# First heads' scores over 66 rows, the first scan and its rows issued ahead of other fills, a table load and the first weights' load

## The chip, the cores and the metric

One Trainium2 chip, one core of it. The time is device microseconds of one execution of the program; before and after are compared by the median of their runs. The profile is of one further execution. Engines: PE (TensorE: MATMUL, and PEld for its weight loads), DVE (VectorE), ACT (ScalarE), POOL (GpSimd), SP (SyncE, which issues most DMAs; rows with SPq or ACTq are DMA issues).

## What is computed

Causal attention with a forget gate (4 batches, 8 heads, 576 positions, 64 wide), then two feed-forward layers on its 2304 rows of 512, each of 2048 hidden columns. Cut to what matters:

```python
scores = matmul(q, k.T) / sqrt(D)
cum    = cumsum(log(clip(f, 1e-4, 1.0)), axis=-1)
scores = where(causal, -1e9, scores + cum[:, None] - cum[None, :])
x      = softmax(scores) @ v          # heads side by side: [2304, 512]
x      = square(relu(x @ w_in)) @ w_out
h      = x @ w_in2
x      = where(h >= 1, h, where(h <= -1, 0, (h + 1)**2 / 4)) @ w_out2
```

## The kernel before

The 2304 columns are worked off in four blocks of 512 to 640. Block 0 holds the first 256 positions of batches 0 and 1. Its heads are taken four at a time: a *group* (`attention32`; groups 0 to 3 make block 0, 4 to 7 block 1). For a group, K and Q of four heads lie transposed in a tile `QK` (two buffers, used in turn): partitions 0 to 63 hold the 64 dimensions, row D = 64 holds cum on the K side and -8 on the Q side, row D + 1 holds 8 on the K side and cum on the Q side, so the score matmul (L819, `s0q` for group 0) adds the decay by itself. All 128 partitions are contracted; the rows beyond are 8 on the K side and 0 on the Q side. These constants are written by `clear` (L726): by DVE for the first buffer, by POOL for the second, in two halves each.

The cum rows come from `setup`: load f (L599), clamp (L603, DVE), Ln (L605, ACT), scan (L607, DVE), each in two pieces, columns 0 to 255 and 256 to 575. Then `first_rows` (L647) copies the first scan's result to rows D and D + 1 of group 0's tile, one DMA on SP's queue and one on ACT's; other groups read it back from DRAM (`cumd`, L642 and L793). ACT loads the table of Exp (L611) after the Ln. A run of matmuls on the identity (L713, `warm`), whose result nobody reads, stands on PE before the scores.

After the scores: masked maximum on DVE (L764, `E0q`), Exp on ACT (L830), scaling by the sum (L853 ACT, L854 DVE), transposes (`tr0q`, L862), products with V (`av0q`, L876), and x written in two float16 pieces (L741, L744, L758).

The feed-forward weights come as 64-bit floats. Each piece of weights (`raw`, L1302; the first two, `raw-2` and `raw-1`, are half pieces) is decoded to float32 by ACT and DVE (L1332, L1336, L1341, L1343), split into two float16 parts (L1398 on ACT or L1399 on DVE, then L758; tile `whl`), and stored for later (`scr`, L1405). The first layer's matmuls are L1423 (`h`), the second's L1587 to L1589 (`acc`).

No order is written out by hand. Every operation is given to a planner with a due time, a guessed cost per engine and, for loads, an earliest time; `Schedule.run` plays the operations through with these costs and picks for each engine the one that is due first, and some operations may go to either of two engines. `improve` repeats this for several weights of the engines' costs and keeps the order with the smallest guessed end; that order is emitted. So a change of one due time can move instructions anywhere. The numbers in two lists are earliest times: `QE` for the groups' QK loads, `RE` for the first raw loads, and `WARM` is the number of warm matmuls.

Of the kernel before, what the change touches and what calls it, by code (L numbers as in the profile page):

```python
# [16 lines left out]
AF = mybir.ActivationFunctionType  # L17
ALU = mybir.AluOpType

B, H, S, D = 4, 8, 576, 64  # L20
DM, DFF = 512, 2048
NT = B * S
P = 128
# [12 lines left out]
HEAD = 256  # L36
# [18 lines left out]
QUAD = 4  # L55
# [1 line left out]

SLAV = [0.0, 0.51, 1.3, 1.3]
SLQK = [0.0, 0.271, 0.412, 0.414]
QE = [0.0, 5.4, 8.66, 11.6]  # L60
VE = [5.5, 6.1]
RE = [1.36, 7.73, 16.0]
LW = 29.1
WARM = 17


def pattern(bits):
# [63 lines left out]
TURN = 0.05  # L131
LEAD = 15.4

WEIGHTS = [{"DVE": x, "POOL": x / 2} for x in (0.4, 0.5, 0.6, 0.8, 1.0)]

class Buf:
    def __init__(self, pool, make, kind=None):
# [25 lines left out]
class Schedule:  # L163
# [175 lines left out]
    def improve(self, pools, rounds):  # L339
        first = [o.due for o in self.ops]  # L340
        best = None
        for weight in WEIGHTS:
            for o, f in zip(self.ops, first):
# [48 lines left out]
def dma_t(nbytes, dram=True, late=0.0):  # L392
    issue = 0.45 if dram else 0.625
    size = nbytes / 380e3
    return issue, size, issue + 0.03, late + 0.1 + 0.35 * size
# [19 lines left out]
def tile_attention_moe_moe(ctx: ExitStack, tc: tile.TileContext, qkv, f, w2, outT, halves, seen=None, bad=None):  # L415
# [19 lines left out]
    sch = Schedule()  # L435
# [35 lines left out]
    def new(tag, name, shape=None, dt=None, kind=None):  # L471
        p, _, sh, d, _ = pools[tag]
        shape = sh if shape is None else shape
        kw = {"padded_shape": sh} if list(shape) != list(sh) and len(shape) == len(sh) and dt is None else {}

        def make():
            if pools[tag][1] is None:
                late_pools()
            return pools[tag][1].tile(shape, dt or d, tag=tag, name=name, **kw)

        return Buf(p, make, kind)
# [8 lines left out]
    else:  # L490
# [13 lines left out]
         early=True)  # L504
# [81 lines left out]
    QK = [new("PT", f"QK{i}", [P, QUAD * 2 * HEAD], F32) for i in range(2)]  # L586
# [3 lines left out]
    def setup():  # L590
        sb = new("xb", "setup", [P, 4 * S], F32)
        fr, lf, cum = (lambda i=i: sb.tile[:H * B, S * i:S * i + S] for i in range(3))
        onesf = lambda: sb.tile[:H * B, 3 * S:4 * S]
        due = -100.0
        G, V_, A = nc.gpsimd, nc.vector, nc.scalar
        tiny_op.append(sch.op(due - 9, {"POOL": (0.05, lambda: G.memset(tiny, 2.0 ** -30))}))
        oh = sch.op(due - 200, {"POOL": (0.05, lambda: G.memset(warm, 0.5))})
        oh = sch.op(due - 200, {"ACT": (1.5, lambda: A.activation(warm, warm, AF.Ln))}, [oh])
        o1 = sch.op(due, {"SP": (dma_t(73728), lambda: nc.sync.dma_start(out=fr(), in_=f))}, bufs=[sb], early=0.0)  # L599
        o2 = sch.op(due - 5, {"POOL": (0.55, lambda: G.memset(onesf(), 1.0))}, bufs=[sb])  # L600
        sch.op(due + 90, {"POOL": (0.05, lambda: G.memset(half, 0.5 * sh[1] ** 0.5))})
        cut = [slice(0, HEAD), slice(HEAD, S)]
        o3 = [sch.op(due, {"DVE": (0.15 + 0.1 * i, lambda c=c: V_.tensor_scalar(  # L603
            fr()[:, c], fr()[:, c], 1e-4, 1.0, op0=ALU.max, op1=ALU.min))}, [o1], [sb]) for i, c in enumerate(cut)]
        o4 = [sch.op(due, {"ACT": (0.32 + 0.05 * i, lambda c=c: A.activation(lf()[:, c], fr()[:, c], AF.Ln))}, [o3[i], oh], [sb])  # L605
              for i, c in enumerate(cut)]
        scan = lambda c, x: V_.tensor_tensor_scan(  # L607
            cum()[:, c], onesf()[:, c], lf()[:, c], x(), op0=ALU.mult, op1=ALU.add)
# [73 lines left out]
        if not halves:  # L682
            due = -30.0
# [7 lines left out]
        if halves:  # L691
# [5 lines left out]
            fill=1.0, base=0, channel_multiplier=1))}, [i1])  # L697
        return o7, zs, ms, i2, o8, first_rows, rows_of_pairs

    cum_op, zs, mask_op, id_op, cumd_op, first_rows, rows_of_pairs = setup()  # L700
    def new_x(name, blk):
        sh = [P, NKC, 2, WIDTH[blk]]
# [4 lines left out]
    def warm_up():  # L707
# [3 lines left out]
        def mms(n):  # L711
            for _ in range(n):
                nc.tensor.matmul(ps.tile[:, :P], ident, ident, start=True, stop=True)  # L713

        sch.op(-90, {"PE": (0.36 * WARM, lambda: mms(WARM))}, [id_op], [ps])

    warm_up()

    def clear(i, half):

        n = QUAD * HEAD
        rows = lambda a, z: QK[i].tile[a:z, n * half:n * half + n]
        kq = lambda a, z, t: rows(a, z).rearrange("p (c t n) -> p c t n", t=2, n=HEAD)[:, :, t, :]
        due = -98 + 2 * i + half
        eng, m = ("POOL", nc.gpsimd) if i else ("DVE", nc.vector)
        fill = lambda out, x: {eng: (n / 1920 + 0.03, lambda: m.memset(out(), x))}  # L726
        kr = sch.op(due, fill(lambda: kq(D, P, 0), 8.0), [], [QK[i]])
        qr = sch.op(due, fill(lambda: kq(D, P, 1), 0.0), [], [QK[i]])
        return [kr, sch.op(due, fill(lambda: kq(D, D + 1, 1), -8.0), [qr], [QK[i]])]

    cleared = {(i, half): clear(i, half) for i in range(2) for half in range(2)}


# [34 lines left out]
    def attention32(g):  # L768
# [1 line left out]
        first = g.blk == 0  # L770
        qk, n = QK[g.i % 2], QUAD * 2 * HEAD
        reg = lambda: qk.tile
        kr = lambda c: reg()[:, 2 * c * HEAD:2 * c * HEAD + HEAD]
        qr = lambda c: reg()[:, 2 * c * HEAD + HEAD:2 * c * HEAD + 2 * HEAD]
        wait = groups[g.i - 2].qk if g.i >= 2 else ()
        src = qkv[g.at:g.at + D * n].rearrange("(p n) -> p n", p=D)
        loads, parts = [], 2 if g.i == 0 else 1
        for i in range(parts):
            c = slice(n // parts * i, n // parts * (i + 1))
            loads.append(sch.op(g.due - 6, {"SP": (dma_t(P * n * 4 // parts), lambda c=c: nc.sync.dma_start(  # L780
                out=reg()[:D, c], in_=src[:, c]))}, wait, [qk], early=QE[g.i] if g.i < len(QE) else None))
        row = g.b * H + g.h
        place = lambda t, c0, c1: reg()[D + t:D + t + 1].rearrange("p (c t n) -> p c t n", t=2, n=HEAD)[:, c0:c1, t, :]
        ready = []
        for i in range(parts):
            c0, c1 = QUAD * i // parts, QUAD * (i + 1) // parts
            if parts == 2:
                if i == 0:
                    rows = [first_rows(row, lambda t=t: place(t, 0, QUAD), -90, [*cleared[0, 0], *cleared[0, 1]], ("SP", "ACT")[t])
                            for t in range(2)]  # L790
                ready += [[loads[i], *rows]] * (c1 - c0)
            else:
                rows = [sch.op(g.due - 4, {"SP": (dma_t(4096), lambda t=t, c0=c0, c1=c1: nc.sync.dma_start(  # L793
                    out=place(t, c0, c1), in_=cumd[row + c0:row + c1, :].rearrange("(o c) n -> o c n", o=1)))},
                    [cumd_op, *wait, *cleared[g.i % 2, 0], *cleared[g.i % 2, 1]], [qk]) for t in range(2)]
                ready += [[loads[i], *rows]] * (c1 - c0)
# [487 lines left out]
    def w_load(s):  # L1284
# [10 lines left out]
        if first:  # L1295
            b = new("raw" if halves else "big", f"raw{s}", [P, 2, 512], U64) if W64 else new("wf", f"wf{s}")
            loads = []
            for pair, layers in first.items():
# [4 lines left out]
                        out=b.tile[:, c], in_=w2[pair].rearrange("p (l n) -> p l n", l=2)[:, c]))},  # L1303
                    [], [b], early=RE[s + LAG] if s <= 0 else V0(s + 2) - 17 - LW))
                for layer in layers:
# [316 lines left out]
    def attend(blk):  # L1622
        if blk:
            xb[blk] = new_x(f"x{blk}", blk)
        for g in groups:
            if g.blk == blk:
                attention32(g)
        if blk in carry:
            buf, (_, off, c0, c1), deps = carry[blk]
            n = c1 - c0  # L1630
            split_x(blk, range(NKC), off, lambda: buf.tile[:, :, :n], n, deps, buf, V[NFC * ATTENTION[blk][0]] + 2)
        for t in tasks:
            if t.blk == blk:
                (attention_pair if halves else attention)(t)
# [600 lines left out]
```

## Time and profile before

| | us |
|---|---|
| median of 3 runs (lowest, highest) | 863.54 (862.9, 866.13) |
| the profiled execution, its own time | 864.67 |
| its span, first to last instruction | 862.8 |
| PE busy in the span | 845.9 (98%) |
| DVE busy | 763.6 (89%) |
| ACT busy | 605.3 (70%) |

A busy time counts the time in which at least one instruction of the engine is under way. Matmuls overlap, so the start of one to the start of the next is the price of one in a row of them, and the duration shown for one is longer than that.

### The profile page before, as it was taken

What the parts mean: (1) busy time and instruction counts of PE and PEld (TensorE: products, weight loads), DVE (VectorE), ACT (ScalarE), POOL (GpSimd) and SP (SyncE); (2) the same over time, 40 slices, a digit from 0 to 9 for tenths busy, and PEclk for the clock granted to TensorE, in tenths of its full rate; (3) what the DMA queues carried; (4) which work ended last, traced back from release to release, by engine and by line L of the source; (5) the groups of instructions that cost most, each with busy time, mean ns of one, the idle gap of its engine ahead of it and who ended that gap; (6) DMA issues with size and microseconds to landing.
All of it is one profiled execution on the core that took longest, in us unless ns stands there. A gap on an engine that the chain in (4) does not pass through costs nothing.

```text
span 862.8 us, 14696 instructions
## 1 busy us (share of the span) xinstructions
PE 845.9 (98%) x4930; PEld 462.7 (54%) x4930; DVE 763.6 (89%) x1882; ACT 605.3 (70%) x1232; POOL 23.8 (3%) x120
## 2 busy tenths in 40 slices
PE   8999999999999999999999999999999999999996
PEld 7644444454444444444446654466556556665553
DVE  8999999999789878989888789986899998999993
ACT  7999988996677667767577577756564566756652
POOL 3000004000000000000000000000000000000000
PEclk9999999999999999999999999999999999999999
DMA  8799997886599998699489988677464454335432
GB/s 258 210 319 323 353 346 230 275 279 222 164 270 226 255 218 241 150 229 257 164 227 264 256 237 208 158 191 161 129 198 156 159 171 159 109 112 168 139 112 76
DMA packets 144841, 180.68 MB, mean 209 GB/s; under 512 B 91670, under 2 KB 96918, under 8 KB 140726
## 3 DMA queue, kind: packets, MB, share of 16 engines
q1 hardware_dynamic: 144750, 179.67, 71.2%
q8 instruction: 40, 0.66, 0.3%
q14 instruction: 43, 0.35, 0.1%
q10 hardware_dynamic: 8, 0.00, 0.0%
HBM read 127.84 MB, written 30.81 MB: 184 GB/s over the span
## 4 chain that ended last, share of the span: by engine, by line
PE 76%; DVE 12%; ACT 6%; DMA 3%; issue 2%; SPq 0%; POOL 0%; DVEq 0%; POOLq 0%; ACTq 0%
PE h L1423 17%; PE acc L1587 8%; PE acc L1589 8%; PE acc L1588 8%; PE h L1972 6%; PE av L1246 3%; PE X L1837 3%; PE Y L1837 2%; PE b L1924 2%; PE b L1926 2%; PE b L1925 2%; DVE wf L1343 2%; PE s L1147 1%; PE s L1146 1%; DMA PT<-PP 1%
## 5 line engine op out<-in xcount | busy, mean ns | idle before, releaser
L1423 PE MATMUL h<-x,whl 128*128 128x512 f16 x912 | 214.3, 379 | 1.0 <-DVE g L1455 1.0
L1423 PEld LDWEIGHTS <-whl 128*128 128x128 f16 x912 | 88.0, 98 | 103.5 <-issue 3.9
L1587 PE MATMUL acc<-gh,whl 128*128 128x512 f16 x312 | 118.3, 379 | 0.0
L1589 PE MATMUL acc<-gl,whl 128*128 128x512 f16 x312 | 118.2, 379 | 0.0
L1588 PE MATMUL acc<-gh,whl 128*128 128x512 f16 x312 | 118.2, 379 | 0.0
L1188 ACT ACTIVATE E<-E,st 128x448 f32<-128x448 f32 (+2 forms) x80 | 54.6, 682 | 33.2 <-DVE st L1186 17.7
L1222 DVE SCALAR_TENSOR_TENSOR PP<-E,st,PP 128x512 f16<-128x512 f32 (+2 forms) x112 | 62.0, 594 | 3.5 <-ACT PP L1218 3.1
L1218 ACT ACTIVATE PP<-E,st 128x512 f16<-128x512 f32 (+2 forms) x112 | 59.4, 588 | 5.9 <-issue 3.5
L1589 PEld LDWEIGHTS <-whl 128*128 128x128 f16 x384 | 37.6, 98 | 45.3
L758 DVE SCALAR_TENSOR_TENSOR gl<-g,gh 128x512 f16<-128x512 f32 x78 | 53.4, 686 | 8.1 <-PE acc L1589 3.2
L1587 PEld LDWEIGHTS <-whl 128*128 128x128 f16 x384 | 37.6, 98 | 40.0 <-issue 3.6
L1588 PEld LDWEIGHTS <-whl 128*128 128x128 f16 x384 | 37.6, 98 | 37.2
L764 DVE CUSTOM_DVE_ANT_0 E<-s,mask 128x288 f32<-128x288 f32 (+1 forms) x96 | 45.4, 509 | 12.1 <-PE s L1147 11.5
L1972 PEld LDWEIGHTS <-wi 128*128 128x128 f16 x336 | 32.9, 98 | 22.8 <-issue 0.9
L1451 ACT ACTIVATE r<-h,half 128x512 f32<-128x512 f32 x40 | 27.1, 678 | 23.6 <-PE h L1423 23.6
L1343 DVE SCALAR_TENSOR_TENSOR wf<-wf,low 128x1024 int32<-128x1024 int32 (+1 forms) x32 | 37.9, 1185 | 2.7 <-ACT low L1340 1.4
L758 DVE SCALAR_TENSOR_TENSOR whl<-wf,whl 128x1024 f16<-128x1024 f32 (+1 forms) x32 | 38.2, 1193 | 1.5 <-ACT whl L1398 1.4
L1332 ACT ACTIVATE wf<-raw 128x1024 f32<-128x1024 f32 (+1 forms) x32 | 35.8, 1119 | 2.0 <-DVE whl L758 1.9
L1641 DVE TENSOR_TENSOR G<-G 128x384 f32<-128x384 f32 x64 | 34.5, 552 | 0.8 <-ACT G L1988 0.4
L1972 PE MATMUL h<-x_last,wi 128*128 128x384 f16 x192 | 33.6, 326 | 0.7 <-DVE G L1996 0.7
L1441 ACT ACTIVATE r<-h 128x512 f32<-128x512 f32 x38 | 22.4, 589 | 13.5 <-PE h L1423 13.1
L1455 DVE SCALAR_TENSOR_TENSOR g<-r,h 128x512 f32<-128x512 f32 x40 | 27.2, 682 | 3.4 <-ACT r L1453 3.1
(620 smaller groups left out, 1924.8 us busy)
## 6 DMA issues: line engine op xcount, KB each, us to landing
raw<-in_w_dram SPq DMA_DIRECT2D x28, 1024.0 KB
whl<-scr SPq DMA_DIRECT2D x56, 512.0 KB
scr<-whl SPq DMA_DIRECT2D x28, 512.0 KB
wo<-scr SPq DMA_DIRECT2D x48, 256.0 KB
k<-in_qkv_dram SPq DMA_DIRECT2D x16, 576.0 KB
wi<-scr SPq DMA_DIRECT2D x23, 256.0 KB
q<-in_qkv_dram SPq DMA_DIRECT2D x16, 320.0 KB
v<-in_qkv_dram SPq DMA_DIRECT2D x16, 320.0 KB
```

Of the source, the lines that this page charges most:

```text
L758: nc.vector.scalar_tensor_tensor(out(), a(), scale, b(), op0=ALU.mult, op1=ALU.subtract, **kw)
L764: return nc.vector.tensor_tensor_reduce(out=out, in0=ps, in1=pairs[:, :n] if q0 is None else mask[:m, OFF - q0:OFF - q0 + n], scale=scale, ...
L1188: o_e.append(sch.op(dc + 0.5, {"ACT": (act_t(e, ptr=1) + 0.14, lambda a=a, e=e, at=at, Ec=Ec: nc.scalar.activation(Ec.tile[:, :e], Ec.tile ...
L1218: nc.scalar.activation(hi, x, AF.Copy, scale=r())
L1222: nc.vector.scalar_tensor_tensor(lo, x, r(), hi, op0=ALU.mult, op1=ALU.subtract)
L1343: return sch.op(due + 4.8, {"DVE": (dve_t(n) + 0.07, lambda: v.scalar_tensor_tensor(yi(), yi(), 3, part(), op0=ALU.logical_shift_left, op1 ...
L1423: nc.tensor.matmul(ps.tile[:, :n], w.tile[:, 0, wi, kc * P:(kc + 1) * P], src.tile[:, kc, xi, :n], start=(kc == 0 and i == 0), stop=(kc == ...
L1587: nc.tensor.matmul(a.tile[:, :n], wh, gh.tile[:, :n], start=(fc == 0), stop=False)
L1588: nc.tensor.matmul(a.tile[:, :n], wl, gh.tile[:, :n], start=False, stop=False)
L1589: nc.tensor.matmul(a.tile[:, :n], wh, gl.tile[:, :n], start=False, stop=(fc == NFC - 1))
L1837: nc.tensor.matmul(bank.tile[:, :n], wt(wi, kk), bt(xi, kk), start=start and z == 0, stop=z == len(todo) - 1, skip_group_check=not start)
L1972: nc.tensor.matmul(ps.tile[:, :n], W0.tile[:, j, wi, kc * P:(kc + 1) * P], src.tile[:, kc, xi, k * n:(k + 1) * n], start=(kc == 0 and i == ...
```

## The change

The score matmuls of the groups read 66 rows of the tile instead of 128, and `clear` fills only what these need: two rows of 8 on the K side and one of -8 on the Q side. `first_rows` is due 30 earlier (-90 to -120); the clamp and Ln of the second piece are due 3 later, and that clamp may not begin before 4.2. The earliest time of `raw-2` goes from 1.36 to 4.6 and that of group 1's QK from 5.4 to 5.7. There are 13 warm matmuls instead of 17. The planner tries one weight instead of five.

```diff
-QE = [0.0, 5.4, 8.66, 11.6]
+QE = [0.0, 5.7, 8.66, 11.6]
-RE = [1.36, 7.73, 16.0]
+RE = [4.6, 7.73, 16.0]
-WARM = 17
+WARM = 13
-WEIGHTS = [{"DVE": x, "POOL": x / 2} for x in (0.4, 0.5, 0.6, 0.8, 1.0)]
+WEIGHTS = [{"DVE": 0.6, "POOL": 0.3}]
...
-        o3 = [sch.op(due, {"DVE": (0.15 + 0.1 * i, lambda c=c: V_.tensor_scalar(
-            fr()[:, c], fr()[:, c], 1e-4, 1.0, op0=ALU.max, op1=ALU.min))}, [o1], [sb]) for i, c in enumerate(cut)]
-        o4 = [sch.op(due, {"ACT": (0.32 + 0.05 * i, ...
+        o3 = [sch.op(due + 3 * i, {"DVE": (0.15 + 0.1 * i, lambda c=c: V_.tensor_scalar(
+            fr()[:, c], fr()[:, c], 1e-4, 1.0, op0=ALU.max, op1=ALU.min))}, [o1], [sb], early=4.2 * i) for i, c in enumerate(cut)]
+        o4 = [sch.op(due + 3 * i, {"ACT": (0.32 + 0.05 * i, ...
...
-        kr = sch.op(due, fill(lambda: kq(D, P, 0), 8.0), [], [QK[i]])
-        qr = sch.op(due, fill(lambda: kq(D, P, 1), 0.0), [], [QK[i]])
-        return [kr, sch.op(due, fill(lambda: kq(D, D + 1, 1), -8.0), [qr], [QK[i]])]
+        return [sch.op(due, fill(lambda: kq(D, D + 2, 0), 8.0), [], [QK[i]]),
+                sch.op(due, fill(lambda: kq(D, D + 1, 1), -8.0), [], [QK[i]])]
...
-        kr = lambda c: reg()[:, 2 * c * HEAD:2 * c * HEAD + HEAD]
-        qr = lambda c: reg()[:, 2 * c * HEAD + HEAD:2 * c * HEAD + 2 * HEAD]
+        kr = lambda c: reg()[:D + 2, 2 * c * HEAD:2 * c * HEAD + HEAD]
+        qr = lambda c: reg()[:D + 2, 2 * c * HEAD + HEAD:2 * c * HEAD + 2 * HEAD]
...
-                    rows = [first_rows(row, lambda t=t: place(t, 0, QUAD), -90, ...
+                    rows = [first_rows(row, lambda t=t: place(t, 0, QUAD), -120, ...
```

What this makes of the order is seen at three places. Line numbers after L724 are one lower in the changed kernel. First DVE, from the program's start to the first masked maximum; before:

```order
L726 MEMSET QK_235 64x2x256 x3
L726 MEMSET QK_235 1x2x256
L603 TENSOR_SCALAR setup<-setup 32x256
L603 TENSOR_SCALAR setup<-setup 32x320
L726 MEMSET QK_235 64x2x256
L607 SCALAR_TENSOR_TENSOR setup<-setup 32x256
L726 MEMSET QK_235 1x2x256
L607 SCALAR_TENSOR_TENSOR setup<-setup 32x320
L1336 TENSOR_SCALAR low_314<-raw-2_264 128x512
```

And with the change (the scan is the row of L607):

```order
L726 MEMSET QK_235 2x2x256
L726 MEMSET QK_235 1x2x256
L726 MEMSET QK_235 2x2x256
L726 MEMSET QK_235 1x2x256
L603 TENSOR_SCALAR setup<-setup 32x256
L607 SCALAR_TENSOR_TENSOR setup<-setup 32x256
L603 TENSOR_SCALAR setup<-setup 32x320
L607 SCALAR_TENSOR_TENSOR setup<-setup 32x320
```

Six fills became four, the first scan stands ahead of the second clamp, and the decode of `raw-2` has gone from here; it stands behind group 0's maxima now. On ACT likewise the first-rows DMA (L647) stands directly behind the first Ln, ahead of the second Ln and of the load of Exp's table, and the first decode row of `raw-2` (L1332 before) stands behind group 0's Exps instead of ahead of them.

Second SP, its first DMAs; before:

```order
L599 DMA setup<-in_f_dram 32x576
L780 DMA QK_235<-in_qkv_dram 64x1024
L1302 DMA raw-2_264<-in_w_dram 128x512
L780 DMA QK_235<-in_qkv_dram 64x1024
L642 DMA cumd<-setup 32x256
L647 DMA QK_235<-setup 1x4x256
L780 DMA QK_273<-in_qkv_dram 64x2048
```

And with the change:

```order
L599 DMA setup<-in_f_dram 32x576
L779 DMA QK_235<-in_qkv_dram 64x1024 x2
L647 DMA QK_235<-setup 1x4x256
L642 DMA cumd<-setup 32x256
L1301 DMA raw-2_291<-in_w_dram 128x512
L779 DMA QK_267<-in_qkv_dram 64x2048
```

The load of `raw-2` has moved behind the rows and `cumd`, which both wait for the scan.

Third PE, ahead of the first scores of group 3 (`s3q`); before:

```order
L862 MATMUL tr2q_551<-ident,E2q_460 128x128
L876 MATMUL av1q_558<-pr1q_525,vt1q 64x256 x2
L876 MATMUL av1q_558<-pr1q_525,vt1q 64x128 x2
L862 MATMUL tr2q_551<-ident,E2q_460 128x128 x2
L862 MATMUL tr2q_571<-ident,E2q_470 128x128 x3
L819 MATMUL s3q_582<-QK_273 128x128
```

And with the change:

```order
L861 MATMUL tr2q_559<-ident,E2q_468 128x128 x3
L861 MATMUL tr2q_570<-ident,E2q_495 128x128
L861 MATMUL tr2q_576<-ident,E2q_486 128x128 x3
L1422 LDWEIGHTS whl-2_402
L1422 MATMUL h_535<-x_393,whl-2_402 128x512
L1422 LDWEIGHTS whl-2_402
L1422 MATMUL h_535<-x_393,whl-2_402 128x512
L1422 LDWEIGHTS whl-2_402
L1422 MATMUL h_535<-x_393,whl-2_402 128x512
L875 MATMUL av2q_587<-pr2q_553,vt2q 64x256 x2
L875 MATMUL av2q_587<-pr2q_553,vt2q 64x128 x2
L818 MATMUL s3q_597<-QK_267 128x128
```

Four transposes, three `h` matmuls and the first half of `av2q` stand ahead of `s3q` that stood behind its first rows. Further on the order differs in places on PE, DVE and ACT through most of the program; on PE the last third is the same row for row.

## Rows read from the trace of the kernel before

**Rows 1.** Busy in two stretches: PE, PEld, DVE, ACT, POOL; then granted clock, DMA share, GB/s.

```profile
8.00:30.00 22.00, 19.31 (x124) 13.50 (x125) 20.12 (x104) 19.35 (x71) 0.00 (x0) 1.00 1.02 288
60.00:100.00 40.00, 40.00 (x205) 19.39 (x204) 38.83 (x81) 37.69 (x68) 0.00 (x0) 1.00 0.96 335
```

**Rows 2.** A piece of the chain that ended last: start, length, what.

```profile
19.63 8.71 DMA QK<-cumd
```

**Rows 3.** Waits of PE from 8 us on: total us, times, longest.

```profile
PE s3q L819 <- DMA QK<-cumd: 1.4, 1, 1.4
PE h L1423 <- DVE g L1455: 1.0, 1, 1.0
```

**Rows 4.** Timeline of PE at the start: start, length, what (three windows).

```profile
1.40 6.56 PE L713 MATMUL warm<-ident 128*128 128x128 f32 x34 [1.40 <-POOL ident L695]
...
4.55 1.70 PE L713 MATMUL warm<-ident 128*128 128x128 f32 x7
...
6.80 1.06 PE L713 MATMUL warm<-ident 128*128 128x128 f32 x8
...
7.80 0.62 PE L819 MATMUL s0q<-QK 128*128 128x128 f32 x3
```

**Rows 5.** Timeline of DVE, 0 to 9.2 us.

```profile
0.91 2.10 DVE L726 MEMSET QK<- 64x512 f32 x4 [0.91 <-PEq L2211]
...
4.66 0.68 DVE L607 TENSOR_TENSOR_SCAN setup<-setup 32x256 f32<-32x256 f32 x1
...
6.01 0.87 DVE L607 TENSOR_TENSOR_SCAN setup<-setup 32x320 f32<-32x320 f32 x1
6.81 0.71 DVE L1336 TENSOR_SCALAR low<-raw-2_264 128x512 uint16<-128x512 uint32 x1
8.80 0.29 DVE L764 CUSTOM_DVE_ANT_0 E0q<-s0q,mask 128x128 f32<-128x128 f32 x1 [1.27 <-PE s0q L819]
```

**Rows 6.** Timeline of ACT, 0 to 9.2 us (ACTq is a DMA issue).

```profile
3.37 0.42 ACT L605 ACTIVATE setup<-setup 32x256 f32<-32x256 f32 x1 [1.12 <-DVE setup L603]
...
4.50 1.28 ACT L611 ACT_TABLE_LOAD   x1
5.37 1.18 ACTq L647 DMA_DIRECT2D QK<-setup  x1
5.79 0.20 ACT L611 ACTIVATE warm<-warm 128x1 f32<-128x1 f32 x1
6.65 0.67 ACT L1332 ACTIVATE wf-2_312<-raw-2_264 128x512 f32<-128x512 f32 x1 [0.66 <-POOL QK L726]
...
9.13 0.40 ACT L830 ACTIVATE E0q<-E0q,st0q 128x128 f32<-128x128 f32 x1 [1.72 <-DVE st0q L764]
```

**Rows 7.** Timeline of SP's DMA issues, 0 to 9.6 us.

```profile
1.84 0.57 SPq L1302 DMA_DIRECT2D raw-2_264<-in_w_dram  x1
...
5.36 0.33 SPq L642 DMA_DIRECT2D cumd<-setup  x1
5.74 0.75 SPq L647 DMA_DIRECT2D QK<-setup  x1
6.54 0.51 SPq L780 DMA_DIRECT2D QK<-in_qkv_dram  x1
```

**Rows 8.** The window 6.4 to 7.8 us, columns as in the first group.

```profile
6.40:7.80 1.40, 1.40 (x13) 1.40 (x12) 1.13 (x2) 0.76 (x2) 1.05 (x3) 1.00 0.03 9
```

**Rows 9.** Timeline of PE and DVE around group 3's first scores.

```profile
25.54 0.87 PE L876 MATMUL av1q<-pr1q,vt1q 128*64 128x256 f32 x8
...
28.47 1.11 PE L819 MATMUL s3q<-QK 128*128 128x128 f32 x6 [1.36 <-DMA QK<-cumd]
...
29.40 0.29 DVE L764 CUSTOM_DVE_ANT_0 E3q<-s3q,mask 128x128 f32<-128x128 f32 x1 [0.48 <-PE s3q L819]
```

**Rows 10.** Timeline of PE at the end: 128 rows, then 11 rows contracted.

```profile
854.66 0.20 PE L1738 MATMUL verdict<-one,sq 128*11 128x1 f32 x2
855.68 0.18 PE L1746 MATMUL verdict<-one,ok 11*1 11x1 f32 x2 [0.82 <-DVE ok L1743]
```

More of the change, by code (lines that the diff above doesn't have):

```diff
@@ L602, in setup @@
         cut = [slice(0, HEAD), slice(HEAD, S)]
-        o3 = [sch.op(due, {"DVE": (0.15 + 0.1 * i, lambda c=c: V_.tensor_scalar(
-            fr()[:, c], fr()[:, c], 1e-4, 1.0, op0=ALU.max, op1=ALU.min))}, [o1], [sb]) for i, c in enumerate(cut)]
-        o4 = [sch.op(due, {"ACT": (0.32 + 0.05 * i, lambda c=c: A.activation(lf()[:, c], fr()[:, c], AF.Ln))}, [o3[i], oh], [sb])
+        o3 = [sch.op(due + 3 * i, {"DVE": (0.15 + 0.1 * i, lambda c=c: V_.tensor_scalar(
+            fr()[:, c], fr()[:, c], 1e-4, 1.0, op0=ALU.max, op1=ALU.min))}, [o1], [sb], early=4.2 * i) for i, c in enumerate(cut)]
+        o4 = [sch.op(due + 3 * i, {"ACT": (0.32 + 0.05 * i, lambda c=c: A.activation(lf()[:, c], fr()[:, c], AF.Ln))}, [o3[i], oh], [sb])
               for i, c in enumerate(cut)]
@@ L788, in attention32 @@
                 if i == 0:
-                    rows = [first_rows(row, lambda t=t: place(t, 0, QUAD), -90, [*cleared[0, 0], *cleared[0, 1]], ("SP", "ACT")[t])
+                    rows = [first_rows(row, lambda t=t: place(t, 0, QUAD), -120, [*cleared[0, 0], *cleared[0, 1]], ("SP", "ACT")[t])
                             for t in range(2)]
```

## The prediction, as it was put on record

> **What bounds the kernel now.** I read the windows of busy time first. From 8 to 30 us PE is busy 19.31 of 22.00 us, DVE 20.12 and ACT 19.35; from 60 to 100 us all three are nearly full, DVE with 38.83 and ACT with 37.69 of 40.00 [rows 1]. The reader is to see that after a start with gaps nobody has spare time: PE can end sooner only if DVE and ACT, which decode the weights meanwhile, are sooner too. Next the chain that ended last: its longest piece at the start is a DMA, the cum rows of group 3, 8.71 us from 19.63 on [rows 2]. The waits of PE say the same: 1.4 us for that DMA and, at the end of the decoding, 1.0 us for DVE's `g` [rows 3]. Then the timeline of the start, engine by engine, since the change begins there. PE runs 34 warm passes (17 matmuls, two passes each) from 1.40 on; seven passes of a window take 1.70 us, eight of a later one 1.06; without the tail of the last, that is 0.213 us from start to start early and 0.112 late, the two levels of 1.2 and 2.4 GHz. `s0q` starts at 7.80 with no idle time ahead of it [rows 4]: the warm passes, not the rows, hold it.
>
> **The change part by part.** The sum is made against the profiled execution, span 862.8 and own time 864.67 us; that is 1.1 above the median, and I carry the difference over to the median of 863.54.
>
> *Warm.* Four matmuls fewer are eight passes. In before the clock has risen by 6.80 [rows 4], after about 25 passes; 26 remain. So those that go are fast ones: 8 x 0.112 = 0.89 us, and `s0q` starts at 6.91.
>
> *Are the rows there by then?* The four fills ahead of the clamp keep their length (1x512 and 64x512 rows cost DVE the same in the order's first four: 2.10 us together [rows 5]). So Ln starts at 3.37 as before and ends at 3.79 [rows 6]; the scan follows at 3.82 instead of 4.66 and ends at 4.50 instead of 5.34 [rows 5]. SP issues its row at 4.53 instead of 5.74, ACT at 4.53 instead of 5.37 [rows 6, 7]. Landing is not shown, but both had landed by 7.80, so at the latest 2.06 and 2.43 us after their issue: by 6.59 and 6.96 now. The warm passes stay last, or nearly. Sooner rows alone are worth nothing; they are what lets the warm passes be cut.
>
> *What queues behind.* On ACT the DMA issue takes 1.18 us [rows 6], to 5.71. The second Ln (0.42 for 256 columns, so about 0.5) and the table load (1.28) and its first use (0.20) follow, to about 7.7. The first Exp can start 0.89 sooner than 9.13 [rows 6], at 8.24: a cover of 0.5, and if it is gone, all that is missing falls on the first Exps. On DVE the second scan (0.87) waits for that second Ln and ends about 7.1, ahead of the first maximum at 8.80 - 0.89 = 7.91 [rows 5].
> In the trace the load that starts at 4.50 ends at 5.78 and the next activation starts at 5.79 [rows 6], so a switch costs its 1.28 and no more; if it took as much again, the first Exps would be 1.28 - 0.5 = 0.8 late.
> The Trainium skill speaks against this place: its page "ScalarE: Activation LUTs", section "What ACT_TABLE_LOAD costs", says that a switch of tables pays a drain of about 1.38 us beside the load's 1.28. By the page the first Exps would be an estimated 0.9 us late and the sum below would come to nothing; the trace does not agree, by the 0.01 us between load and activation.
>
> *raw-2.* On SP it was issued at 1.84 [rows 7]; now it is behind the scan, the row (0.75) and `cumd` (0.33): about 5.6. Group 1's QK, which stood at 6.54 [rows 7], then goes at about 6.2, and all behind it are not later either. The first decode rows of raw-2 lay in time that DVE and ACT had free: 0.71 us on DVE ahead of an idle 1.27, 0.67 on ACT ahead of 1.72 [rows 5, 6]. Now they stand among group 0's softmax, where both engines are busy. So DVE begins 0.89 sooner with 0.71 more to do, ACT 0.89 sooner with 0.67 more: net 0.18 and 0.22, **0.2 us** gained for the pair, not 0.9. A cast of these weights that goes from DVE to ACT while scalings go the other way changes the pair's sum little; I take nothing.
>
> *DMA.* From 6.40 to 7.80 the DMA engines are idle (share 0.03) [rows 8]. raw-2 (0.52 MB; at the 288 GB/s of the stretch [rows 1] 1.8 us) now uses that gap of 1.4. The queue behind is 0.4 us later if it uses the whole gap, 1.8 if none of it. I take 0.5, since its issue ends well before the gap does.
>
> *Group 3.* Its rows land at 28.33 after 8.71 us in the queue [rows 2], and PE idles 1.36 [rows 9]. With the change PE has three `h` matmuls (0.22 us each), four transposes (a 0.112 pass each) and half of `av2q` (at most the 0.87 of `av1q`'s [rows 9]) ahead of `s3q`: 1.9 to 2.0 us that stood behind. It is PE's gap that this fills; what DVE gains is its own wait there, 0.48 [rows 9]. I take **0.5 us**, with 0 and 1.36 as ends. The 0.5 us by which the landing may be later is covered by the 1.9.
>
> *66 rows.* No f32 score pass of the trace contracts fewer than 128 rows. The bounds: no change at all, or time in proportion to rows, which over 64 passes of 0.112 and 64 of twice that would be 21.5 us x 62/128 = 10 us gained. The nearest rows have one column: two passes over 128 rows take 0.20 us, two over 11 rows 0.18 [rows 10]. That is the same but for hundredths, so I take nothing. POOL's and DVE's dropped fills lay in free time and give nothing either. The one weight is what before's order was made with already.
>
> *Sum.* 0.2 + 0.5 = 0.7 us: the profiled 864.67 becomes 864.0, the median 863.54 becomes **862.8**. PE's own 0.89 and the gap are not added, because DVE and ACT bound the stretch behind.
>
> **The rivals.**
> (1) PE gets all of it: the warm passes and the whole gap, 0.89 + 1.36 = 2.25 us, so 861.3. For it: PE is full from 60 us on; against it: so are DVE and ACT [rows 1].
> (2) Slower, by raw-2: if it uses nothing of the idle gap, all DMAs behind are 1.8 us later, group 3 lands at 30.1, and PE's work moved ahead just covers it, but the decoding of the next weights is as late. 862.8 + 1.8 = 864.6. It decides from 28.47 + 1.9 = 30.4 on for `s3q`'s start. Against it: the gap is there to be used.
> (3) The clock rises later. The warm run is now hardly longer than what the clock needed before. Then the first scores run at the low level: eight passes that lose 0.10 each and eight that lose 0.2, up to 2.4 us, so 862.8 + 2.4 = 865.2. Against it: the scores follow without a gap, and the rise, which lies ahead of 6.80 [rows 4], is also ahead of the warm run's end at 6.9. The Trainium skill, "TensorE: Matmul & The Clock Gate", Part 1, says that the moment of the rise is one of time and not of a count of matmuls, and that it varies from run to run; by it such executions would occur now and then.
> (4) Exp's table is late: if a switch takes as much again as its load, the 0.8 us above are lost, 863.6. Against it: the 0.01 us behind the load [rows 6]. This is what the page's drain would do.
> (5) The order further on. It differs almost to the end, and single waits there are of 1.0 us [rows 3] and more; two new ones give 864.8, two that go 860.8. No row tells which.
> (6) The change does nothing: if `s0q` waits for the rows as long as for warm passes before, 863.5.
>
> **How the numbers follow.** The forecast 0.42; (1) 0.20; (2) 0.11; (3) 0.05; (4) 0.04; (5) slower 0.07, faster 0.06; (6) 0.05. The likeliest gives 862.8. Leaving out a tenth on either side, the range goes from 860.4 (between (1) and the better end of (5)) to 865.3 (beyond (2) and (3)). About 0.5%, 4.3 us, is what a measurement can tell from no change: faster than 859.2 would take more than PE's gaps before 30 us (22.00 - 19.31 = 2.7) and the warm passes together, or shorter score passes: 0.06. Slower than 867.9 would take (2), (3) and (5) at once: 0.05. The rest, 0.89, is no change that can be told.
>
> **What would show it.** The warm passes number 26 and `s0q` starts at 6.9 to 7.0, with its passes 0.112 apart from the start. The first scan ends at 4.5. The second table load is over by 7.8 and the first Exp starts near 8.2. `s3q` starts at 28.5 to 29.5 with a PE wait well under 1.36. A score pass keeps its 0.112. Between 60 and 140 us DVE and ACT do the same rows at most 1 us sooner. Wrong would be: `s0q` after 7.3, warm passes that end at the low level, `s3q` after 30, a first Exp that waits for the table, or a new wait of PE over 2 us behind 140.

## The result, and the profile after

| | before | after |
|---|---|---|
| median, us (lowest to highest, runs) | 863.22 (862.88 to 866.13, 4) | 875.34 (874.41 to 877.17, 4) |
| the profiled execution: own time, span | 864.67, 862.8 | 874.82, 873.0 |
| its mean granted clock | 0.998 | 0.985 |

The changed kernel is slower: ratio 1.0135, 95% interval 1.0118 to 1.0153, about 12 us. The forecast was 862.8 us, a range of 860.4 to 865.3, and no change that can be told.

First the two stretches and the short window whose rows of before are [rows 1, 8], in the kernel after; the columns are those of [rows 1]:

```profile
8.00:30.00 22.00, 18.46 (x74) 13.51 (x73) 13.57 (x74) 14.32 (x51) 0.00 (x0) 0.64 0.98 262
60.00:100.00 40.00, 40.00 (x203) 19.81 (x202) 38.42 (x74) 37.60 (x69) 0.00 (x0) 1.00 0.92 315
...
6.40:7.80 1.40, 1.40 (x9) 1.35 (x8) 0.81 (x1) 1.39 (x2) 0.00 (x0) 1.00 0.60 155
```

PE is busy nearly as long from 8 to 30 us as before (18.46 and 19.31), but it does 74 passes in place of 124, and DVE and ACT, full before, get 5 to 7 us less done. The seventh number of the first row shows what goes with it: the mean granted clock is 0.64, not 1.00. From 60 us on all is as it was. The same in finer stretches, after, and then before in the first two of them:

```profile
8.00:14.00 6.00, 4.03 (x21) 2.44 (x19) 5.67 (x33) 5.54 (x22) 0.00 (x0) 1.00 0.94 225
14.00:34.00 20.00, 18.43 (x70) 13.62 (x71) 10.60 (x57) 10.52 (x37) 0.00 (x0) 0.50 0.88 242
34.00:36.00 2.00, 2.00 (x15) 1.06 (x13) 0.88 (x4) 1.85 (x7) 0.00 (x0) 0.88 0.50 102
36.00:60.00 24.00, 23.01 (x135) 13.34 (x134) 22.62 (x74) 22.88 (x62) 0.00 (x0) 1.00 0.66 225
```

```profile
8.00:14.00 6.00, 5.18 (x26) 3.11 (x25) 5.10 (x29) 4.87 (x20) 0.00 (x0) 1.00 1.01 291
14.00:34.00 20.00, 18.13 (x125) 13.36 (x126) 18.99 (x93) 18.04 (x66) 0.00 (x0) 1.00 1.02 303
```

For 20 us, from 14 to 34, the clock stands at the low level (0.50 of 2.4 GHz, so 1.2) while PE is busy 18.43 of 20.00 us. Ahead of it, from 8 to 14, PE was busy 4.03 of 6.00 us, where before had 5.18. Now PE's timeline after, to be held against [rows 4, 9]:

```profile
1.41 5.91 PE L713 MATMUL warm<-ident 128*128 128x128 f32 x26 [1.41 <-POOL ident L695]
...
4.13 3.18 PE L713 MATMUL warm<-ident 128*128 128x128 f32 x14
...
7.12 2.81 PE L818 MATMUL s0q<-QK 66*128 66x128 f32 x16
10.48 1.39 PE L861 MATMUL tr0q<-ident,E0q 128*128 128x128 f32 x6 [0.55 <-DVE E0q L853]
12.38 0.70 PE L861 MATMUL tr0q<-ident,E0q 128*128 128x128 f32 x3 [0.51 <-DVE E0q L853]
14.97 1.54 PE L875 MATMUL av0q<-pr0q,vt0q 128*64 128x256 f32 x8 [1.89 <-DMA vt0q<-in_qkv_dram]
...
28.82 2.77 PE L818 MATMUL s2q<-QK 66*128 66x128 f32 x8
...
34.33 0.89 PE L1422 MATMUL h<-x,whl-2_402 128*128 128x512 f16 x3
...
39.69 1.58 PE L818 MATMUL s3q<-QK 66*128 66x128 f32 x8
```

and of before, the first products with group 0's values, the scores of group 1 and the last of group 2:

```profile
12.70 1.40 PE L876 MATMUL av0q<-pr0q,vt0q 128*64 128x256 f32 x4 [0.15 <-ACT pr0q L741]
...
15.53 2.86 PE L819 MATMUL s1q<-QK 128*128 128x128 f32 x16
...
21.19 1.56 PE L819 MATMUL s2q<-QK 128*128 128x128 f32 x8
```

The last 14 warm passes take 3.18 us, about 0.212 from start to start without the tail of the last (0.42): they run at the low level to the end, and the scores behind them at the high one. `s0q` starts at 7.12 instead of 7.80, then PE waits three times, at last 1.89 us for group 0's values. Before, `av0q` waited 0.15 us there, for ACT and not for a DMA. 16 score passes over 66 rows take 2.81 us where the clock is high, and 16 over 128 rows took 2.86: the rows don't change the time of a pass at one clock. But the last eight of `s2q` take 2.77 against 1.56. The clock is back with the first `h` (34.33), and `s3q` starts 11.2 us later than before.

What the other engines did at the start, with SP's queue first, then DVE, then ACT ([rows 5 to 7] for before):

```profile
4.61 0.75 SPq L647 DMA_DIRECT2D QK<-setup  x1
5.41 0.48 SPq L642 DMA_DIRECT2D cumd<-setup  x1
5.93 0.42 SPq L1301 DMA_DIRECT2D raw-2_291<-in_w_dram  x1
6.39 0.51 SPq L779 DMA_DIRECT2D QK<-in_qkv_dram  x1
6.95 0.58 SPq L799 DMA_DIRECT2D vt0q<-in_qkv_dram  x1
```

```profile
3.90 0.68 DVE L607 TENSOR_TENSOR_SCAN setup<-setup 32x256 f32<-32x256 f32 x1 [0.56 <-POOL QK L726]
...
8.12 0.29 DVE L763 CUSTOM_DVE_ANT_0 E0q<-s0q,mask 128x128 f32<-128x128 f32 x1 [0.91 <-PE s0q L818]
...
12.50 0.46 DVE L1335 TENSOR_SCALAR low<-raw-2_291 128x512 uint16<-128x512 uint32 x1
12.84 0.45 DVE L1340 TENSOR_SCALAR low<-raw-2_291 128x512 uint16<-128x512 uint16 x1
...
13.66 0.55 DVE L853 TENSOR_SCALAR E0q<-E0q,st0q 128x128 f32<-128x128 f32 x2
```

```profile
4.61 1.18 ACTq L647 DMA_DIRECT2D QK<-setup  x1
5.84 0.47 ACT L605 ACTIVATE setup<-setup 32x320 f32<-32x320 f32 x1 [2.05 <-issue]
6.33 1.28 ACT L611 ACT_TABLE_LOAD   x1
7.62 0.20 ACT L611 ACTIVATE warm<-warm 128x1 f32<-128x1 f32 x1
8.46 0.40 ACT L829 ACTIVATE E0q<-E0q,st0q 128x128 f32<-128x128 f32 x1 [0.63 <-DVE st0q L763]
```

A piece of the chain that ended last shows what became of the values' load (start, length):

```profile
6.95 7.89 DMA vt0q<-in_qkv_dram
```

It was issued at 6.95, sooner than before, and landed at 14.84; before, `av0q` ran at 12.70 and waited for no DMA. And the scaling of the fourth head (13.66) stands behind the two decode rows of `raw-2`.

So there are two suspects: scores over 66 rows, and the gaps that the new order leaves on PE. They could each do it alone, or only together.

### The profile page after: what moved, and what is told of

It reads as the page before. It is cut to its first block, busy times and chain, and to the rows that moved or that the text cites. A ratio compares the mean times of both kernels' runs of the same rounds, so it can differ in the third digit from the quotient of the medians.

```text
span 873.0 us, 14666 instructions
## 1 busy us (share of the span) xinstructions
PE 854.5 (98%) x4922; PEld 468.9 (54%) x4922; DVE 752.3 (86%) x1861; ACT 620.4 (71%) x1253; POOL 20.7 (2%) x118
## 4 chain that ended last, share of the span: by engine, by line
PE 81%; DVE 10%; DMA 3%; ACT 3%; issue 1%; SPq 0%; ACTq 0%; DVEq 0%
PE h L1422 22%; PE acc L1586 9%; PE acc L1587 9%; PE acc L1588 9%; PE h L1971 4%; PE av L1245 3%; DMA PT<-PP 2%; PE X L1836 2%; DVE c L1640 2%; DVE G L1640 1%; PE b L1923 1%; PE s L1146 1%; PE s L1145 1%; PE b L1925 1%; PE b L1924 1%
## 5 line engine op out<-in xcount | busy, mean ns | idle before, releaser
L1836 PEld LDWEIGHTS <-si 128*128 128x128 f16 x216 | 21.1, 98 | 15.6 <-issue 1.7
```

What stands on the lines that cost most here:

```text
L1836: nc.tensor.matmul(bank.tile[:, :n], wt(wi, kk), bt(xi, kk), start=start and z == 0, stop=z == len(todo) - 1, skip_group_check=not start)
```

## The experiments

Each row is the median of the run's own executions. The kernel before was measured beside them, with medians of 863.8 us beside e1 to e4, 863.7 beside e5 to e8, 864.05 beside e9 to e12 and 865.1 beside e13 and e14; the ratios are to these. Granted clocks of single executions below are means over the whole execution. The rows and waits of a run are those of its one profiled execution.

| run | us (lowest to highest, runs) | ratio to before, 95% interval |
|---|---|---|
| e1_rows128 | 870.33 (865.85 to 871.86, 4) | 1.0087 (1.0070 to 1.0103) |
| e2_before66 | 864.15 (863.07 to 865.70, 10) | 1.0006 (0.9996 to 1.0015) |
| e3_vt_first | 874.05 (869.54 to 876.56, 4) | 1.0122 (1.0081 to 1.0163) |
| e4_vt_rows128 | 866.59 (866.32 to 867.64, 5) | 1.0040 (1.0026 to 1.0054) |
| e5_warm66 | 868.04 (865.47 to 870.03, 9) | 1.0046 (1.0032 to 1.0059) |
| e6_raw_first | 865.78 (863.07 to 870.63, 10) | 1.0028 (1.0009 to 1.0048) |
| e7_two_groups | 868.11 (866.82 to 868.98, 5) | 1.0047 (1.0032 to 1.0062) |
| e8_pad | 869.64 (868.71 to 870.81, 4) | 1.0068 (1.0051 to 1.0085) |
| e9_raw_rows128 | 866.17 (863.67 to 868.41, 12) | 1.0016 (1.0000 to 1.0033) |
| e10_five_weights | 871.70 (869.93 to 872.68, 4) | 1.0074 (1.0052 to 1.0097) |
| e11_raw_warm17 | 865.60 (864.10 to 873.87, 10) | 1.0034 (1.0010 to 1.0058) |
| e12_warm17 | 877.25 (872.92 to 878.32, 4) | 1.0130 (1.0102 to 1.0158) |
| e13_gap128 | 866.29 (863.08 to 868.60, 10) | 1.0015 (0.9998 to 1.0033) |
| e14_gap66 | 873.54 (872.94 to 875.04, 4) | 1.0099 (1.0066 to 1.0133) |

### Rows alone, order alone (e1, e2)

e1 gives the changed kernel its 128 rows back (the fills add the same constant to every score, which the softmax removes); e2 gives the kernel before 66 rows and keeps its order.

```diff
-        kr = lambda c: reg()[:D + 2, 2 * c * HEAD:2 * c * HEAD + HEAD]
+        kr = lambda c: reg()[:, 2 * c * HEAD:2 * c * HEAD + HEAD]
...
```

> The changed kernel with the scores over all 128 rows again: the same two fills per half cover rows 64 to 127 (8 on the K side, -8 on the Q side, which adds the same constant to every score and leaves the softmax as it is), every instruction at its place. Theory A, the 66 rows: passes over 66 rows do not hold or lift the clock as passes over 128 do. It expects the wait of 1.9 us for vt0q to stay, the clock to be back at the high level within some 4 us of PE's next run of passes, or not to fall, and 862 to 867 us. Theory B, the wait: PE's gap of 2 us before av0q drops the clock, and the rows do not matter. It expects the low level from 14 to 34 us again and 874 to 876 us.

> The kernel before, in its own order, with its three fills and its score passes cut to 66 rows. Theory A expects the clock to fall somewhere between 8 and 35 us though no wait is new, and 867 to 876 us. Theory B expects the clock to stay at the high level from 7 us on and 862.5 to 864.5 us.

e2 is as fast as before, and its clock stays high:

```profile
16.00:24.00 8.00, 8.00 (x58) 6.30 (x56) 7.75 (x47) 7.89 (x32) 0.00 (x0) 1.00 1.06 370
```

So 66 rows alone do no harm in the old order; theory A, the rows, failed here. e1 gains 5 us on the changed kernel but fits neither theory's range: its runs have a mean clock of 0.997 once (865.85 us, the profiled one, where no stretch to 40 us is low) and 0.993 or 0.994 three times (869.6 to 871.9), where the changed kernel has 0.984 to 0.987. The new order costs something with 128 rows too.

### The late values (e3, e4)

The first values' load goes ahead of `raw-2` on SP, with 66 rows (e3) and with 128 (e4).

```diff
-        o_v = sch.op(g.due, {"SP": (dma_t(P * vn * 4), lambda: nc.sync.dma_start(
...
+        o_v = sch.op(g.due, {"SP": (dma_t(P * vn * 4), (lambda: turned["raw"]()) if g.i == 0 else load_v)}, [], [vt], early=VE[g.i] if g.i < len(VE) else g.due - 4)
...
+                    "SP": (dma_t(size, late=2.5 if s < 0 else 0.0), (lambda: turned["vt0"]()) if s == -LAG else load_w)},
```

> The changed kernel with two loads in each other's place on SP: vt0q is issued where raw-2 was, and raw-2 where vt0q was; 66 rows, everything else at its place. The wait of 1.9 us for vt0q should be gone or below 0.5. Theory A expects the clock to fall all the same in the first 35 us and 868 to 875 us. Theory B expects it to stay high and 861 to 864 us.

> Both: vt0q ahead of raw-2, and 128 rows. Both theories expect no fall of the clock before the end and 861 to 863.5 us, which would be what the change gives without the clock; if it is still over 866, neither theory is the whole cause.

In e3 the wait for values is gone and the clock falls all the same; the 1.3 us that it gains lie within its own spread. In e4 it doesn't fall in any run (0.997 or 0.998). First e3, then e4:

```profile
12.00:16.00 4.00, 3.45 (x16) 2.23 (x17) 2.69 (x10) 2.40 (x9) 0.00 (x0) 0.52 1.06 313
...
12.00:16.00 4.00, 2.86 (x20) 2.05 (x20) 3.04 (x12) 3.27 (x11) 0.00 (x0) 1.00 1.10 333
```

Between e3 and e4 only the rows differ: **7.5 us**. PE waits less for the first transposes in e3 (1.6 us for `tr0q`, 0.6 for `tr1q`) than in e4 (below), so here the rows decide not only how long the clock stays low but whether it falls. e4's own expectation failed: it is still 2.8 us over the kernel before, at a full clock. That is a second loss, which neither theory has. Its waits of PE show where some of it is (total us, times, longest); before waited 0.7 us for `tr0q` and not for `tr1q`:

```profile
PE tr0q L867 <- DVE E0q L859: 1.9, 3, 0.9
...
PE tr1q L867 <- DVE E1q L859: 1.1, 1, 1.1
```

### Do 66 rows count for less? (e5)

The kernel before with its warm passes over 66 rows of the identity:

```diff
-                nc.tensor.matmul(ps.tile[:, :P], ident, ident, start=True, stop=True)
+                nc.tensor.matmul(ps.tile[:, :P], ident[:D + 2, :], ident[:D + 2, :], start=True, stop=True)
```

> The kernel before, but its 17 warming passes multiply 66 rows of the identity instead of 128; nothing else is changed. Theory A (a pass over 66 rows counts for less towards the granted clock than one over 128, though it takes the same time): the rise to the high level comes clearly later than in the kernel before (6.7 us there) or the scores of the first group run at the low level with a pass twice as long; 2 to 6 us slower, 866 to 870. Rival (the rows of a pass do not matter to the clock, and the changed kernel's fall comes from the gaps of its new order alone): the rise is where it was, within 1 us, and the time is 863 to 864.5.

The timeline of its PE, and the busy times of its first 8 us:

```profile
1.40 7.62 PE L713 MATMUL warm<-ident 66*128 66x128 f32 x34 [1.40 <-POOL ident L695]
8.82 4.12 PE L819 MATMUL s0q<-QK 128*128 128x128 f32 x16
...
0.00:8.00 8.00, 6.60 (x31) 6.60 (x32) 5.83 (x11) 4.62 (x8) 6.29 (x29) 1.00 0.58 153
```

All 34 passes run at the low level (34 x 0.213 = 7.2 us and the last one's tail), where in [rows 4] the clock rose during them and they took 6.56. It rose only during the 128-row scores behind, whose 16 passes take 4.12 us and not 2.80 to 2.86. The granted clock reads 1.00 in the first 8 us all the same: ahead of the first rise the column says nothing, and the level is read from the spacing of the passes. So the theory is borne out at the place where nothing else differs: 34 passes over 66 rows, back to back, didn't raise the clock here.

### The weights' load at its old place (e6, e9, e11)

e6 is the changed kernel with the two numbers of before below, and with them the planner's order changes on every engine, not only where the load stands; e9 is e6 with 128 rows; e11 is e6 with four warm matmuls more, both in e6's order.

```diff
-QE = [0.0, 5.7, 8.66, 11.6]
-RE = [4.6, 7.73, 16.0]
+QE = [0.0, 5.4, 8.66, 11.6]
+RE = [1.36, 7.73, 16.0]
```

> The changed kernel with the first weights' load back at its old place on SP's queue (and with it the decode back ahead of the first scores on DVE); 66 rows, 13 warming passes and the early scan stay. Theory: the late load does the damage twice, by DVE's decode among the first heads' work and by holding the first values up, and the gaps that these leave on PE let the granted clock fall. Then the waits of the first transposes and of av0q fall below 0.6 us together, the clock stays high through 14 to 34 us, and the time is 861.5 to 864.5. Rival (with 66 rows any order but the old one falls, since the scores themselves hold the clock too weakly): the low stretch of 15 to 20 us is still there and the time is 872 to 876. Between: a short fall, 865 to 870.

> The changed kernel with the first weights' load at its old place (as in e6_raw_first) and scores over 128 rows: neither the late decode nor 66 rows are left, only the early scan, 13 warming passes and the planner's new order behind them. Theory (the clock costs the rest of e6_raw_first's loss, 865.8 with runs from 863.1 to 870.6): a steady granted clock of 0.997 and 863 to 865, runs close together. Rival (the order further on costs the 2 to 3 us by itself, as it did in e4_vt_rows128): 865.5 to 867 at a steady clock.

> e6_raw_first (the first weights' load at its old place, 66 rows) with 17 warming passes instead of 13, its order kept: the four stand where PE waited 0.95 us for the first rows, so they cost nothing. Theory (the four passes of 128 rows help to hold the clock through the first group, so without them 66 rows let it fall in some runs): runs close together at a granted clock of 0.996 to 0.998, 863.5 to 865. Rival (the falls of e6_raw_first have nothing to do with the warming passes): as spread as there, some runs at 0.991 to 0.995, 865 to 867.

e6 takes back most of the loss, 875.3 to 865.8, between the two theories: its waits for the first transposes are down to 0.7 us in total and the profiled execution keeps the clock, while its runs reach from 863.1 (clock 0.998) to 870.6 (0.991). The mean clock is no sure price: two of its runs took 864.7 and 865.4 us at 0.993 and 0.994. With 128 rows (e9) the clock is steady, 0.995 to 0.998, but the median is no better than e6's: the rival's range is met. The 1.4 (by the ratio) to 2.1 us (by the medians) that are left come at a steady clock. The order and the wait of `s0q` for its rows, which follows, are the candidates; neither was tried alone. Neither theory of e11 holds: eight of its ten runs lie together, 864.1 to 867.0 at 0.996 to 0.998, and two fell (873.0 and 873.9, clock 0.990 and 0.985). Four matmuls of warming don't protect 66 rows.

In e6, the wait of `s0q`:

```profile
PE s0q L818 <- DMA QK<-setup: 0.8, 1, 0.8
```

`s0q` starts at 7.86 there, though its rows' DMAs are issued at 4.60, as in the changed kernel, where it started at 7.12. With the weights' load ahead, the first rows landed later, and the start that the change had wanted was not had in these runs.

### Where the 128 rows matter, and filled gaps (e7, e8)

e7 is e4 with 128 rows in the first two groups only; e8 is e3 with four extra 128-row matmuls on the identity ahead of each of the first four sets of transposes, 16 in all. A matmul is two passes, so these are 32 passes; the expectation prices 16.

```diff
-        kr = lambda c: reg()[:, 2 * c * HEAD:2 * c * HEAD + HEAD]
+        kr = lambda c: reg()[:P if g.i < 2 else D + 2, 2 * c * HEAD:2 * c * HEAD + HEAD]
...
```

```diff
                 for to in places:
...
+                for _ in range(4 if g.i == 0 and 0 in places else 0):
+                    nc.tensor.matmul(tr.tile[:, :P], ident, ident, start=True, stop=True)
```

> The kernel with values ahead of the weights and scores over 128 rows (866.6), but only the first two groups' scores contract 128 rows; from the third group on they contract 66. Theory (the clock is lost in the sparse first group and a half, and passes over 66 rows can hold it once PE is dense): no fall, mean granted clock 0.997, 866 to 868. Rival (66 rows let it fall wherever they stand): the clock falls some time after the third group's scores begin, near 20 us, and the time lies between 868 and 874.

> The kernel with values ahead of the weights and scores over 66 rows (874.0, clock low from 12.2 to 32.6 us), and four more passes over 128 rows of the identity ahead of each of the first group's four sets of transposes, written into the transposes' own tile and overwritten by them: PE works where it waited for DVE. Their cost is 16 x 0.11 = 1.8 us at most, and nothing where they fill the waits. Theory (gaps on PE plus 66 rows let the clock fall): filled gaps keep it high or shorten the low stretch, 865.5 to 869. Rival (66 rows alone, the gaps do not matter): still low for 20 us, 874 to 876.

e7 keeps the clock in three of five runs (0.997, 0.998) and loses a little in two (0.994); 868.1 lies just over the theory's range and just inside the rival's. The rows of the first two groups give back some 6 of the 7.5 us, so they matter most. In e8 the fall comes later and is shorter, and 869.6 is just over what the theory gave:

```profile
16.00:20.00 4.00, 3.32 (x22) 2.35 (x20) 3.16 (x19) 3.68 (x14) 0.00 (x0) 1.00 1.03 323
20.00:24.00 4.00, 3.57 (x17) 3.19 (x18) 2.94 (x19) 3.10 (x12) 0.00 (x0) 0.69 1.03 391
24.00:28.00 4.00, 4.00 (x17) 2.46 (x17) 2.66 (x15) 2.18 (x10) 0.00 (x0) 0.50 0.86 193
28.00:32.00 4.00, 4.00 (x18) 2.16 (x17) 2.11 (x10) 3.19 (x11) 0.00 (x0) 0.53 0.44 111
```

The clock, which in e3 went at 12 us, holds here until after 20. 4.4 us are gained on e3, with 32 passes added: with the gaps filled by 128-row passes, the same 66-row scores cost less. Whether the filling does it or the 128 rows of what fills, e8 can't tell.

### Five weights, four warm matmuls (e10, e12)

e10 is e4 with the planner's five weights; e12 the changed kernel with 17 warm matmuls, order kept.

```diff
-WEIGHTS = [{"DVE": 0.6, "POOL": 0.3}]
+WEIGHTS = [{"DVE": x, "POOL": x / 2} for x in (0.4, 0.5, 0.6, 0.8, 1.0)]
```

```diff
-        sch.op(-90, {"PE": (0.36 * WARM, lambda: mms(WARM))}, [id_op], [ps])
+        sch.op(-90, {"PE": (0.36 * WARM, lambda: mms(WARM + 4))}, [id_op], [ps])
```

> The kernel with values ahead of the weights and scores over 128 rows (866.6, clock steady), but the planner may choose among the five weights of the kernel before again. If the one weight of the changed kernel picked a worse order further on: 863.5 to 865.5. Rival (the 2.8 us over the kernel before come from DVE's decode among the first heads' work, which both orders have): 866 to 868, with waits of the first transposes for DVE of 1.5 us or more.

> The changed kernel with 17 warming passes instead of 13, its order kept: the first scores start up to 0.43 us later. Theory (the gaps ahead of av0q and of the transposes let the clock fall, 8 us after the warming passes): the fall stays, 873 to 876. Rival (the four passes alone tip it): the low stretch is gone or under 8 us long, 866 to 870.

Both expectations for e10 failed: another order, sparser still, and the clock fell with 128 rows too (from 13 to 20 us). So the one weight isn't what costs, and 128 rows are no full protection.

```profile
12.00:16.00 4.00, 2.48 (x12) 1.26 (x14) 1.67 (x8) 2.62 (x8) 0.00 (x0) 0.64 1.06 316
16.00:20.00 4.00, 4.00 (x19) 2.31 (x18) 1.66 (x7) 2.19 (x7) 0.00 (x0) 0.51 1.01 313
```

e12 is as slow as the changed kernel (877.25 us, a little over its theory's range): the four matmuls are not the cause. Its `av0q` waits only 0.3 us for the values, so with 66 rows that long wait isn't needed for the fall either.

### One gap in the old order (e13, e14)

What was open is whether a gap and 66 rows are enough without the rest of the new order. In both kernels no engine's order is touched but SP's: group 0's values are loaded behind `raw-1`. e13 has before's 128 rows, e14 the 66 of e2.

```diff
+                if s == 1 - LAG:
+                    turned["raw"] = load_w
...
+                    "SP": (dma_t(size, late=2.5 if s < 0 else 0.0), (lambda: turned["vt0"]()) if s == 1 - LAG else load_w)},
```

> The kernel before, every engine's order kept, but the first group's values are loaded behind the second weights on SP's queue instead of ahead of them, so that av0q waits some 1.5 to 3 us for them as in the changed kernel. Theory (a gap needs scores over 66 rows to cost the clock for long): the granted clock stays high or falls for under 8 us, 863.5 to 867. Rival (a gap of this size lets the clock fall for 20 us whatever the rows): 870 to 876.

> The same late values in the kernel before with scores over 66 rows (e2_before66, which kept the clock at 864.2). Theory: the clock falls near 12 to 14 us, 7 us after its rise, and stays low until passes over 128 rows are dense again at h, 24 us or later: 868 to 874. Rival (what tipped the changed kernel lies elsewhere in its order): no fall, at most the gap's own 1 to 3 us, 864 to 867.

The waits, e13 and then e14:

```profile
PE av0q L880 <- DMA vt0q<-in_qkv_dram: 2.4, 1, 2.4
...
PE av0q L880 <- DMA vt0q<-in_qkv_dram: 2.2, 1, 2.2
```

What follows, first e13:

```profile
16.00:20.00 4.00, 4.00 (x20) 3.25 (x18) 1.45 (x7) 2.80 (x8) 0.00 (x0) 0.57 1.03 405
20.00:34.00 14.00, 13.45 (x95) 9.42 (x93) 13.58 (x70) 13.43 (x50) 0.00 (x0) 1.00 0.85 260
```

and e14:

```profile
16.00:24.00 8.00, 8.00 (x30) 5.92 (x32) 3.52 (x22) 4.96 (x17) 0.00 (x0) 0.50 0.82 319
24.00:34.00 10.00, 10.00 (x41) 7.51 (x38) 5.99 (x35) 4.80 (x18) 0.00 (x0) 0.50 0.46 113
```

The gap takes the clock down in both. With 128 rows it is back after some 4 us, and the kernel is 1 us over the kernel before beside it, which is not clear of noise (0.9998 to 1.0033). With 66 rows PE is busy 18.00 of 18.00 us and stays at the low level through them: 873.5, some 8 us over. So the rows of the scores behind the gap decide whether it costs about 1 us or 8.

Taken together: 66 rows in the old, dense order cost nothing (e2), a gap with 128 rows next to nothing (e13), both together 8 us (e14). A gap of 2.2 to 2.4 us brought the clock down with either number of rows; where the waits are short, it fell with 66 and held with 128 (e3, e4). That is no full rule: in e10 it fell with 128 rows and waits of at most 1.1 us, and in e11 with 66 rows in two runs of ten.

No kernel here beats the kernel before; e2 equals it.

## Why the prediction was wrong

The times, e4, e3 and the changed kernel in a row, split the 12 us: 2.8 for the new order at a full clock (e4 over before), 7.5 for 66 rows (e3 over e4), 1.3 for the late values (after over e3, within e3's spread). By way of e1 it is 2.8, then 3.7 for the late values and 5.0 for the rows, though e1's own runs lie 6 us apart. The rows and the waits work on each other, so neither has one price.

- **66 rows: the step that failed.** "That is the same but for hundredths, so I take nothing." For a pass at one clock this holds (2.81 us for 16 against 2.86). The Trainium skill, "TensorE: Matmul & The Clock Gate", section "Why this matters for your kernels", says the same of a single matmul that contracts 32 rows, and the trace agrees. But I priced the pass and not what it does to the granted clock. Measured in its place: 5.0 us (after over e1) to 7.5 (e3 over e4) in the new order, nothing in the old (e2).
- **Rival (3)** saw a clock that rises late, behind the warm passes, for at most 2.4 us. Its sign came: the warm passes end at the low level, which the prediction had named as a sign of being wrong. But the clock rose as the scores began, and they ran at the high level, so it cost nothing. That it could fall again once risen wasn't among my cases, and its "the scores follow without a gap" looked at the first gap only.
- **What queues behind raw-2: wrong by its waiter.** The issues stood as worked out, at 5.93 and 6.39 for 5.6 and 6.2, and the DMA engines used the idle window (share 0.60 for 0.03). But I followed one load, group 3's rows, with "0.5 us later". The first to be waited for was `vt0q`, the second load behind: it landed at 14.84, at least 2.1 us later than before. The rival's 1.8 was nearer than the 0.5 I took.
- **The decode of raw-2: wrong in sign.** A gain of 0.2 us was worked out from the sum of DVE's work. In place of it the rows at 12.50 and 12.84 stand ahead of the fourth head's scaling, and PE waits for transposes: 3.0 us in e4 (`tr0q` and `tr1q`), 0.7 in before and in e6, which decode early. That the decode alone makes the difference was not tried, since e6 has another order throughout. A sum over a stretch hides which row stands ahead of which.
- **Warm: a little off.** The eight passes that went were priced as fast ones, 0.89 us; all that are left were slow, and `s0q` gained 0.68 (it starts at 7.12, not 6.91).
- **Scan, rows, table: right.** The scan ended at 4.58 (4.50) and the rows were there for `s0q`. The table's load ended at 7.61 and the next activation stood at 7.62; the first Exp started at 8.46 and waited for DVE. Rival (4) is out.
- **Group 3's wait is gone** as forecast, but in the changed kernel that shows nothing: `s3q` stands 11 us later, at 39.69, where a start after 30 was to be a sign of being wrong. In e4, with the clock high, `s3q` starts at 30.6 and waits for no DMA either. What DVE was to gain, 0.5, can't be seen in either.
- **The order further on**, left at plus or minus 2: e9, which has neither the late load nor 66 rows, measured 1.0016 (1.0000 to 1.0033), so at most some 3 us of loss, in an order of its own. Which rows of it cost that was not tried one by one.

What stays open is why e6 and e11 lose the clock in some runs and not in others, though PE waits for little there, and why e10 lost it with 128 rows.

## What to carry to other kernels

Price a matmul with fewer rows twice: by its pass, and by whether the kernel has a sparse stretch ahead of it in which the clock can fall, because passes over few rows may leave it low for as long as they last, as here. When a load is moved back, follow each load behind it to its first waiter, not only the one that is waited for now. When work moves from an idle stretch into a busy one, look for the row that it now stands ahead of.

## What the runs showed of the hardware

- PE full with 66-row passes, transposes and 64-column products had the low clock for 18 us on end (e14, 18.00 of 18.00 busy, 0.50); with 128-row scores in the same order it was back after some 4 us (e13).
- In one order, with single waits of PE of at most 1.1 us, the clock fell near 12 us with 66-row scores (e3, 0.52 from 12 to 16) and stayed high with 128 rows (e4, 0.997 or 0.998 in five runs).
- 34 warm passes over 66 rows took 7.62 us, over 128 rows 6.56 in the kernel before and, as the moment of the rise varies, 5.42 in e2.
- One wait of PE of 2.4 us behind a dense start was followed by a fall of the clock with 128 rows too (e13).
